# The second layer of a mixture of experts in Strassen form for its last 1024 tokens, with weights split once and kept in DRAM

## The chip, the cores and the metric

The kernel runs on one core of one Trainium2 chip. The metric is the device time of one launch in microseconds (us): a median of 831.98 us over three runs (831.94 to 832.38). The profiled execution, which all rows below come from, took 832.07 us; its span (first to last instruction) is 830.3 us, so 1.77 us lie around the span.

## The reference

Attention over 4 batches of 576 tokens and 8 heads of 64 (half of the heads with a local mask, half with a strided one) gives x, 2304 tokens by 512. Then four experts, each a two-layer network, are summed with weights p per token:

```
x = attention(q, k, v)                      # 2304 x 512, fp32
p = domain_probs / (domain_probs.sum(-1) + 1e-9)
for e in range(4):
    h = max(x @ w1[e], 0)                   # w1[e]: 512 x 1024
    out += p[:, e:e+1] * (h @ w2[e])        # w2[e]: 1024 x 512
```

All of it is fp32. p is not negative, so p times max(h, 0) can be formed before the second layer or applied behind it.

## The kernel before

**Three parts of the tokens.** The 2304 tokens are worked in three parts: the first 384 (beside the attention), a middle part of 896 and a last part of 1024. Each part goes through eight units (expert e, half f of the 1024 hidden columns), so a unit is x times a 512 x 512 block of w1, a relu, and a product with a 512 x 512 block of w2. The last part takes the units in the order 6, 0, 1, 2, 3, 4, 5, 7.

**Split operands.** TensorE (PE) multiplies in float32r. To keep fp32 accuracy each operand is split into a high part (an ACT copy to float32r, `split` L631) and a low part (source minus high, on DVE or POOL, kind "VP" in the plan), and each product is three passes: high by high, high by low, low by high.

**First layer, middle and last part: Strassen.** `plan_unit` (L841) makes seven block products (a11, s1, s2, a12, s3, a22, s4 with b11, t1, t2, b21, t3, t4, b22) instead of eight; each is done for two halves f of its 256 rows by `product` (L829, six matmuls of 448 or 512 columns), so 14 products and 84 matmuls a unit. The weights' combinations and splits are made by DVE, POOL and ACT from the raw block (`plan_w1` L662), in the middle part and again in the last. Some results are copied out of PSUM by ACT (`copy_u`), added by DVE, then relu'd and split into h high (ACT) and h low (DVE).

**Second layer: plain.** `plan_mm2` (L723): a tile of 128 tokens is 12 matmuls of 512 columns with h as the stationary operand (L706); behind it DVE does acc = psum * p + acc (`accumulate`, L715), one instruction a tile. The last part has eight such tiles a unit. At the end each acc goes to DRAM.

**What sets the order.** Every instruction is added to a plan (`Plan`, L33) with an engine, an estimated time, the values read and written, and a priority; `Plan.walk` makes a list schedule, and the engines' instruction streams are written in that order. Engines run their streams in order. PE's products and tiles keep the order in which they are added. "VP" instructions go to DVE or POOL, whichever the plan thinks ends first. Where DVE and POOL overlap, the plan's rule (`took`, L188) charges DVE half of what is left of POOL's instruction:

```
d += min(x / 2, d) if e == "DVE" else min(x, d) * 0.2
```

The SP queue issues all weight loads (`plan_load`: one raw block of 1 MB for w1 and one for w2 a unit) and the outputs, also in order. PSUM has eight banks: four named mo, two sc, two ps.

Of the kernel before, what the change touches and what calls it, by code (L numbers as in the profile page):

```python
# [8 lines left out]
F32 = mybir.dt.float32  # L9
# [23 lines left out]
class Plan:  # L33
# [273 lines left out]
def attn_moe_kernel(  # L307
# [8 lines left out]
    w2: bass.AP,  # L316
    c_masks: bass.AP,
    out: bass.AP,
):
    nc = tc.nc  # L320
    B, H, S, D = 4, 8, 576, 64
    NT, DM = out.shape
    E, _, F = w1.shape
    P = 128
    NKD = DM // P
# [30 lines left out]
    psums = const.tile([P, NTT], F32, name="psums")  # L356
    wz = const.tile([P, 512], BF16, name="wz")

    wq = {n: (big.tile([P, 2, 256], F32R, name=n + "h"), big.tile([P, 2, 256], F32R, name=n + "l")) for n in QUART[:3] + ("s3",)}
    w2h = [big.tile([P, DM], F32R, name=f"w2h{i}") for i in range(NKF)]  # L360
    w2l = [big.tile([P, DM], F32R, name=f"w2l{i}") for i in range(NKF)]
    raws = {1: big.tile([P, NKD, FH], F32, name="raw1"), 2: big.tile([P, NKF, DM], F32, name="raw2")}
    acc = [big.tile([P, DM], F32, name=f"acc{i}") for i in range(TB // P)]
    xr = {"r2": [big.tile([P, TBS[1]], F32, name=f"xr2{c}") for c in range(NKD)]}

    one = tc.tile_pool(name="one", bufs=1)
    op = one.__enter__()
# [294 lines left out]
    def plan_w1(z, step, plain):  # L662
# [16 lines left out]
        combine(t(0), A12, t(1), ["raw1", "ws1"], "ws0", z + 6 * step)  # L679
        plan_quarter(t(0), "ws0", "s4", z + 6 * step)  # L680


    PASS = [(i, c) for i in range(3) for c in range(NKD)]
    PASS0 = [(i, c) for c in KORD for i in range(3)]
# [89 lines left out]
    def open_first():  # L774
        att.__exit__(None, None, None)
        p = ctx.enter_context(tc.tile_pool(name="late1", bufs=1, side="right", reuse_waits="tile"))
        for nm in XOPS:
            xq[nm] = [[p.tile([P, TM], F32R, name=f"{nm}{h}{j}") for j in range(2)] for h in "hl"]
        for nm in ("s1", "s2", "s4"):
            wq[nm] = (p.tile([P, 2, 256], F32R, name=nm + "h"), p.tile([P, 2, 256], F32R, name=nm + "l"))  # L780
        for i in range(3):
            tmp["s", i] = p.tile([P, 2, 256], F32, name=f"tmp{i}")

    def open_second():
        one.__exit__(None, None, None)
        p = ctx.enter_context(tc.tile_pool(name="late2", bufs=1, reuse_waits="tile"))
        late["h"] = [[p.tile([P, TB], F32R, name=f"h{j}{i}") for i in range(NKF)] for j in range(2)]
        late["u"] = [p.tile([P, TM], F32, name=f"u{i}") for i in range(4)]
        late["c"] = [p.tile([P, TM], F32, name=f"c{i}") for i in range(2)]

    def plan_x(part, z, step):

# [48 lines left out]
    def plan_unit(part, u, first, last, z):  # L841
# [31 lines left out]
        for n, (a, b, keys, first_in) in enumerate(SEQ):  # L873
            for f in range(2):
                key = keys[f]
                zz = z + (2 * n + f) * PM
                need = [a + "h", a + "l"] + [f"{b}{h}{j}" for h in "hl" for j in range(2)]
                add("PE", PM, lambda a=a, b=b, f=f, key=key, first_in=first_in: product(a, b, f, key, first_in, TH),
                    need, [key], zz, key if first_in else None, True, 6 * TH)
                ze = zz + PM  # L880
                if n == 0:
                    copy_u("p1", f, key, ze)
                elif n == 2:
                    copy_u("u2", f, key, ze)
# [34 lines left out]
        plan_pair(n)  # L919
    add("SP", 0.4, load_pr, (), ["prs"], 8, xfer=((0.1, 128),))  # L920
    add("DVE", 1.0, normalize, ["prs"], ["pr"], 30)

    for u in range(NU):
        z = Z0 + ZU * u
# [17 lines left out]
    for part, seq in ((1, first_order), (2, second_order)):  # L942
        PM = pm_of(part)
        w1_at = 14 * PM + 2 * PT * (TBS[part - 1] // P)
        for i, u in enumerate(seq):
            if part == 1 and i == 0:
                plan_w1(z, 2 * PM, False)
            elif i > 0:
                plan_load(1, u, z - w1_at + 9)
                plan_w1(z, 2 * PM, True)  # L950
                plan_load(2, u, z - w1_at + 17)
                plan_w2(z + 14 * PM)
# [96 lines left out]
```

## Time and profile before

| what | value |
|---|---|
| median of 3 runs | 831.98 us |
| profiled execution | 832.07 us, span 830.3 us |
| first part with the attention | 0 to 210.0 us |
| middle part, 8 units of 36.1 us | 210.0 to 498.7 us |
| last part, 8 units of 40.95 us | 498.7 to 826.3 us |
| PE busy | 822.8 us of the span |
| DVE, ACT, POOL busy | 496.3, 322.4, 213.2 us |
| moved by DMA | 70.6 MB |

Busy time is that of an engine's instructions; idle time of an engine that nobody waits for costs nothing. In the rows below L with a number is the line of the kernel before.

### The profile page before, as it was taken

The page shows a single profiled execution, that of the slowest core. Times are in us where ns is not written, and L with a number is a line of the kernel's source. Part 1 is how long each engine was busy: PE and PEld are TensorE (multiplying, and loading weights), DVE is VectorE, ACT ScalarE, POOL GpSimd, SP SyncE. Part 2 cuts the span into 40 slices and gives each one's busy share as a digit, 9 for nine tenths or more (in the row PEclk, how much of TensorE's full clock was granted, in tenths as well). Part 3 has the DMA queues.
Part 4 walks back from the last instruction along what each step waited for, and adds up shares of the span by engine and source line. Part 5 has one row for each costly group of instructions (what it writes and reads, how often), then busy time and mean ns, then how long its engine had stood idle before and what let it go on. Part 6 is the DMA issues. An engine that isn't in the chain of part 4 may idle for free.

```text
span 830.3 us, 13407 instructions
## 1 busy us (share of the span) xinstructions
PE 822.8 (99%) x5492; PEld 702.5 (85%) x5495; DVE 496.3 (60%) x773; ACT 322.4 (39%) x607; POOL 213.2 (26%) x185
## 2 busy tenths in 40 slices
PE   8999999999999999999999999999999999999998
PEld 5888988998988888898888888888888888888886
DVE  6977877855646465574647685464646464646342
ACT  3644546542514334161433525161515151515130
POOL 5421134841223131231315271121211111111000
PEclk9999999999999999999999999999999999999999
DMA  9675532343012111121211110111112020201002
GB/s 341 238 282 180 202 143 95 106 147 114 28 49 101 51 52 51 51 58 52 94 51 51 51 71 19 52 54 48 58 44 69 33 80 23 89 12 52 1 8 95
DMA packets 33230, 70.60 MB, mean 85 GB/s; under 512 B 1936, under 2 KB 2320, under 8 KB 33168
## 3 DMA queue, kind: packets, MB, share of 16 engines
q1 hardware_dynamic: 33024, 69.66, 24.0%
q8 instruction: 43, 0.70, 0.3%
q14 instruction: 19, 0.16, 0.1%
q10 hardware_dynamic: 144, 0.08, 0.0%
HBM read 65.01 MB, written 4.72 MB: 84 GB/s over the span
## 4 chain that ended last, share of the span: by engine, by line
PE 96%; DMA 2%; DVE 1%; POOL 0%; ACT 0%; issue 0%; ACTq 0%
PE mo L706 28%; PE mo L834 17%; PE ps L706 10%; PE sc L706 10%; PE ps L834 9%; PE sc L834 9%; PE mo L690 8%; PE ps L551 1%; PE sc L469 1%; PE ps L559 1%; DMA raw<-in_w 1%; PE ps L523 1%; PE sc L464 1%; DMA both<-c_masks 0%; DVE pmS L486 0%
## 5 line engine op out<-in xcount | busy, mean ns | idle before, releaser
L706 PE MATMUL mo<-w2h,h 128*128 128x512 f32 (+1 forms) x488 | 159.2, 387 | 0.0
L634 ACT ACTIVATE w2h<-raw 128x512 fp32r<-128x512 f32 x88 | 54.6, 631 | 249.5 <-PE ps L706 104.6
L715 DVE SCALAR_TENSOR_TENSOR acc<-mo,pr,acc 128x512 f32<-128x512 f32 x74 | 55.2, 746 | 88.1 <-PE mo L706 87.4
L706 PEld LDWEIGHTS mo<-w2h,h 128*128 128x128 f32 x488 | 91.4, 188 | 18.7
L706 PE MATMUL mo<-w2l,h 128*128 128x512 f32 (+1 forms) x244 | 94.6, 388 | 0.0
L697 DVE SCALAR_TENSOR_TENSOR h<-c,h 128x448 fp32r<-128x448 f32 (+1 forms) x96 | 90.9, 977 | 6.0 <-ACT h L694 3.6
L706 PE MATMUL ps<-w2h,h 128*128 128x512 f32 x240 | 78.8, 389 | 0.0
L706 PE MATMUL sc<-w2h,h 128*128 128x512 f32 (+1 forms) x240 | 77.8, 386 | 0.0
L635 POOL TENSOR_TENSOR w2l<-raw,w2h 128x512 fp32r<-128x512 f32 x24 | 32.7, 1366 | 151.1 <-ACT w2h L634 150.5
L706 PE MATMUL mo<-w2h,hs 128*128 128x512 f32 x192 | 63.3, 397 | 0.0
L694 ACT ACTIVATE h<-c 128x448 fp32r<-128x448 f32 (+1 forms) x96 | 55.6, 601 | 13.3 <-DVE c L866 11.7
L706 PEld LDWEIGHTS mo<-w2l,h 128*128 128x128 f32 x244 | 45.8, 188 | 9.3
L706 PEld LDWEIGHTS ps<-w2h,h 128*128 128x128 f32 x240 | 45.0, 188 | 9.3
L706 PEld LDWEIGHTS sc<-w2h,h 128*128 128x128 f32 x240 | 44.9, 188 | 9.1
L635 DVE TENSOR_TENSOR w2l<-raw,w2h 128x512 fp32r<-128x512 f32 x64 | 45.5, 742 | 9.5 <-ACT w2h L634 9.5
L635 POOL TENSOR_TENSOR s3l<-tmp,s3h 128x512 fp32r<-128x512 f32 x14 | 18.3, 1305 | 115.3 <-ACT s3h L634 107.2
L853 ACT ACTIVATE u<-mo 128x448 f32<-128x448 f32 (+1 forms) x48 | 27.4, 572 | 51.4 <-PE mo L834 50.8
L706 PE MATMUL ps<-w2l,h 128*128 128x512 f32 x120 | 46.7, 389 | 0.0
L706 PE MATMUL sc<-w2l,h 128*128 128x512 f32 (+1 forms) x120 | 46.3, 386 | 0.0
L706 PEld LDWEIGHTS mo<-w2h,hs 128*128 128x128 f32 x192 | 36.0, 188 | 7.9
L715 DVE SCALAR_TENSOR_TENSOR acc<-ps,pr,acc 128x512 f32<-128x512 f32 x27 | 20.3, 751 | 36.7 <-PE ps L706 36.6
L866 DVE TENSOR_TENSOR c<-mo,u 128x448 f32<-128x448 f32 (+1 forms) x48 | 31.1, 648 | 16.0 <-issue 8.1
(279 smaller groups left out, 1710.1 us busy)
## 6 DMA issues: line engine op xcount, KB each, us to landing
raw<-in_w SPq DMA_DIRECT2D x44, 1024.0 KB, 5.2
qkS<-in_qk_strided SPq DMA_DIRECT2D x16, 329.0 KB, 7.7
vstL<-in_v_local SPq DMA_DIRECT2D x8, 640.0 KB, 8.2
out<-acc SPq DMA_DIRECT2D x17, 256.0 KB, 2.0
vstS<-in_v_strided SPq DMA_DIRECT2D x8, 384.0 KB, 8.1
qkL<-in_qk_local SPq DMA_DIRECT2D x8, 336.0 KB, 6.9
qkL<-in_qk_local SPq DMA_DIRECT2D x8, 272.0 KB, 6.3
out<-acc SPq DMA_DIRECT2D x2, 128.0 KB, 1.7
```

What stands on the lines that cost most here:

```text
L464: nc.tensor.matmul(s[64 * h + 32 * i:64 * h + 32 * i + 32, o:o + W], qkv[a, t:t + 32], qkv[a, t + nq + 1:t + nq + 1 + W], start=True, stop ...
L469: nc.tensor.matmul(s[a, o:o + W], lhsT, rhs, start=True, stop=True)
L634: add("ACT", 0.62, lambda: nc.scalar.activation(out=hi(), in_=src(), func=AF.Copy), need, [name + "h"], z)
L635: add("VP", VP, lambda e: engine(e).tensor_tensor(out=lo(), in0=src(), in1=hi().bitcast(F32), op=ALU.subtract), need + [name + "h"], [name ...
L690: nc.tensor.matmul(pt[:, 0:TA], w[:, c % 2, (f % 2) * P:(f % 2) * P + P], (xl if i == 1 else xh)[c], start=j == 0, stop=j == 11)
L694: nc.scalar.activation(out=dst(), in_=src(), func=AF.Relu)
L697: nc.vector.scalar_tensor_tensor(out=dst(), in0=src(), scalar=0.0, in1=hi().bitcast(F32), op0=ALU.max, op1=ALU.subtract)
L706: nc.tensor.matmul(pt, ht[f][:, ts], wt[f][:, cs], start=j == 0, stop=j == 11)
L715: nc.vector.scalar_tensor_tensor(out=a, in0=pt, scalar=sc, in1=a, op0=ALU.mult, op1=ALU.add)
L834: nc.tensor.matmul(pt, wq[a][i == 2][:, j, f * P:f * P + P], xq[b][i == 1][j][:, 0:TH], start=bool(first) and n == 0, stop=True, skip_grou ...
L853: add("ACT", TH / 1200 + 0.18, lambda: nc.scalar.activation(out=late["u"][i][:, 0:TH], in_=held[key][:, 0:TH], func=AF.Copy), [key, "late2 ...
L866: add("DVE", TH / 960 + 0.14, lambda: nc.vector.tensor_tensor(out=late["c"][c][:, 0:TH], in0=held[key][:, 0:TH], in1=late["u"][i][:, 0:TH] ...
```

## The change

**Middle part.** The split weight operands are now stored. After each unit's seven w1 operands are split, SP writes each (high and low together, 512 KB) to DRAM (`plan_keep1`, not for unit 6, whose operands stay in place). `plan_keep2` does the same for w2: three operands are written straight from the split w2 block (rows of 1 KB), and the other four are formed by four "VP" combinations and four splits through two buffers wv0 and wv1. So a middle unit has 14 more DMAs, 8 more "VP" instructions and 4 more ACT copies (unit 6 seven DMAs fewer).

**Last part.** No raw weights are loaded and none are split. SP reads the seven w1 operands of a unit back into place (`reload`) and the seven w2 operands through a ring of four buffers (`plan_ring`). The second layer is Strassen as well, with w2 as the stationary operand, so the output is turned (512 x 1024, turned back on the host): 14 products of six matmuls (`plan_o`) instead of eight tiles of twelve. h becomes q = max(h, 0) * p on DVE, with p spread over all partitions (`pb`, by DMA from a turned copy `dp` in DRAM, once an expert), and q's seven combinations are formed and split (`plan_t`). Each product of the second layer is added to acc by DVE. `TURN` interleaves: a turn is the h products of one unit, two of the next unit's ("next P2", "next s1"), and then the seven o products.

```diff
+    wt = {n: big.tile([P, 2, 2, 256], F32R, name=n) for n in QUART[:3] + ("s3",)}
+    wq = {n: (t[:, 0], t[:, 1]) for n, t in wt.items()}
...
+    def plan_keep1(u, z):
+        for n, nm in enumerate(QUART):
+            add("SP", 0.4, lambda nm=nm: nc.sync.dma_start(out=d1[u, nm], in_=wt[nm].bitcast(F32)), [nm + "h", nm + "l"], [f"d1{u}{nm}"],
+                z + n, xfer=((1.45, 128),))
...
+        def keep(n, nm):
+            v = n % 2
+            split(t((0, 1, 2, 0)[n]), f"ws{(0, 1, 2, 0)[n]}", lambda: late["wv"][v][:, :, 0], lambda: late["wv"][v][:, :, 1], f"wv{v}", z + n * step)
+            add("SP", 0.4, lambda: nc.sync.dma_start(out=d2[u, nm], in_=late["wv"][v].bitcast(F32)), [f"wv{v}h", f"wv{v}l"], [f"d2{u}{nm}"],
+                z + n * step + 2, xfer=((1.45, 128),))
...
+    STEPS = {"P2": ("a12", "b21", "b", 1), "s1": ("s1", "t1", "c", 1), "P1": ("a11", "b11", "a", 1), "s4": ("s4", "b22", "c", 0),
+             "s2": ("s2", "t2", "a", 0), "s3": ("s3", "t3", "a", 0), "a22": ("a22", "t4", "a", 0)}
+    TURN = ("h P1", "h s4", "h s2", "next P2", "h s3", "next s1", "h a22", "o P1", "o s1", "o s2", "o s4", "o s3", "o P2", "o a22")
...
+            if nm:
+                i = late[nm, f]
+                add("DVE", DD, lambda: nc.vector.tensor_tensor(out=q(), in0=src(), in1=late["u"][i], op=ALU.add),
+                    [key, f"u{i}", "late3"], [tok], zz)
+            from_q = bool(nm)
+            add("DVE", DD, lambda: nc.vector.scalar_tensor_tensor(
+                out=q(), in0=q() if from_q else src(), scalar=0.0, in1=late["p"][:, c * TH2:c * TH2 + TH2], op0=ALU.max, op1=ALU.mult),
...
+            elif step == "s3":
+                sub(q[0, 0, j], q[1, 1, j], q[0, 0, j], z)
+                put(q[0, 0, j], "t2", j, z)
+                put(q[1, 1, j], "b22", j, z + 2 * dz)
+                sub(q[0, 1, j], q[1, 1, j], q[0, 1, j], z + 4 * dz)
+                put(q[0, 1, j], "t3", j, z + 4 * dz)
...
+            key = ({"a": "sc", "b": "ps", "c": "mo"}[kk], "o" + kk, u, f)
...
+            add("PE", dz, lambda f=f, key=key: product(
+                [late["ring"][slot][:, :, h] for h in range(2)], late["T"][b], f, key, first_in, TH2),
+                need, [key], zz, key if first_in else None, True, 6 * TH2)
...
+                add("DVE", DD, lambda i=i, key=key: nc.vector.tensor_tensor(
+                    out=acc[i], in0=held[key][:, 0:TH2], in1=acc[i], op=ALU.add), [key], tok, zz + dz)
...
-            elif part == 2:
-                plan_x(2, z, 2 * PM)
-            plan_unit(part, u, i == 0, i == NU - 1, z)
-            z += w1_at
...
+        plan_keep2(u, z + 14 * PM, 2 * PM)
+        z += w1_at
+    plan_x(2, z, 2 * pm_of(2))
...
+    plan_second()
```

**DVE in the last part.** Before, the stretch of a unit from the second half of its h products to the first tiles; c is an h product with a parked one added, h0 and h1 are h's high and low parts, mo, ps and sc are PSUM banks.

```order
L697 SCALAR_TENSOR_TENSOR h12_2771<-c0_2777,h02_2767 128x512
L697 SCALAR_TENSOR_TENSOR h13_2772<-c1_2778,h03_2768 128x512
L697 SCALAR_TENSOR_TENSOR h12_2771<-mo_5249,h02_2767 128x512
L697 SCALAR_TENSOR_TENSOR h13_2772<-ps_5261,h03_2768 128x512
L866 TENSOR_TENSOR c0_2777<-mo_5270,u2_2775 128x512
L866 TENSOR_TENSOR c1_2778<-ps_5279,u3_2776 128x512
L697 SCALAR_TENSOR_TENSOR h10_2769<-c0_2777,h00_2765 128x512
L697 SCALAR_TENSOR_TENSOR h11_2770<-c1_2778,h01_2766 128x512
L715 SCALAR_TENSOR_TENSOR acc0_94<-mo_5382,pr_72,acc0_94 128x512
```

After, from s3's first h product to the first read of an o product (acc0 from sc); q is max(h, 0) * p, v a parked product, T... the o operands (l low, h high).

```order
L928 TENSOR_TENSOR q110_5072<-ps_5659,v2_5057 128x512
L931 SCALAR_TENSOR_TENSOR q110_5072<-q110_5072,pb_5065 128x512
L928 TENSOR_TENSOR q111_5073<-ps_5667,v3_5058 128x512
L960 TENSOR_TENSOR q000_5066<-q110_5072,q000_5066 128x512
L931 SCALAR_TENSOR_TENSOR q111_5073<-q111_5073,pb_5065 128x512
L956 TENSOR_TENSOR Tt2l0_5092<-q000_5066,Tt2h0_5090 128x512
L960 TENSOR_TENSOR q001_5067<-q111_5073,q001_5067 128x512
L956 TENSOR_TENSOR Tb22l1_5085<-q111_5073,Tb22h1_5083 128x512
L931 SCALAR_TENSOR_TENSOR q100_5070<-ps_5659,pb_5065 128x512
L956 TENSOR_TENSOR Tt2l1_5093<-q001_5067,Tt2h1_5091 128x512
L931 SCALAR_TENSOR_TENSOR q101_5071<-ps_5667,pb_5065 128x512
L1005 TENSOR_TENSOR acc0_80<-sc_5798,acc0_80 128x512
```

Before, an instruction that reads a bank had at most two instructions with both inputs in SBUF ahead of it in such a stretch; now seven stand ahead of the read of sc.

**POOL beside it.** Before, POOL's whole unit in the last part:

```order
L635 TENSOR_TENSOR s3l_83<-tmp2_2199,s3h_82 128x512
L635 TENSOR_TENSOR a22l_81<-raw1_92,a22h_80 128x512
L635 TENSOR_TENSOR s4l_2196<-tmp0_2197,s4h_2195 128x512
L639 TENSOR_TENSOR tmp1_2198<-tmp0_2197,raw1_92 128x512
L635 TENSOR_TENSOR w2l1_89<-raw2_93,w2h1_85 128x512
```

After, POOL's whole turn; the first needs q110, which is the second DVE row above.

```order
L960 TENSOR_TENSOR q010_5068<-q110_5072,q010_5068 128x512
L956 TENSOR_TENSOR Tb22l0_5084<-q110_5072,Tb22h0_5082 128x512
L956 TENSOR_TENSOR Tt3l0_5096<-q010_5068,Tt3h0_5094 128x512
L960 TENSOR_TENSOR q011_5069<-q111_5073,q011_5069 128x512
L956 TENSOR_TENSOR Tt3l1_5097<-q011_5069,Tt3h1_5095 128x512
L956 TENSOR_TENSOR Tb21l0_5080<-q100_5070,Tb21h0_5078 128x512
L960 TENSOR_TENSOR q100_5070<-q100_5070,q000_5066 128x512
L960 TENSOR_TENSOR q101_5071<-q101_5071,q001_5067 128x512
```

POOL has gone from five instructions a unit, spread over it, to eight in a row behind s3.

**SP in the middle part.** Before, SP issued two loads a unit and nothing else there:

```order
L624 DMA raw1_92<-in_w1 128x4x512
L624 DMA raw2_93<-in_w2 128x4x512
```

After, one unit (d1 and d2 are the DRAM copies of the w1 and w2 operands):

```order
L634 DMA raw2_202<-in_w2 128x4x512
L695 DMA d11s2_101<-s2_2297 128x1024
L695 DMA d11a12_98<-a12_77 128x1024
L695 DMA d11s3_102<-s3_79 128x1024
L695 DMA d11a22_99<-a22_78 128x1024
L695 DMA d11s4_103<-s4_2298 128x1024
L634 DMA raw1_201<-in_w1 128x4x512
L715 DMA d21s1_149<-wv0_2877 128x1024
L715 DMA d21s2_150<-wv1_2878 128x1024
L715 DMA d21s3_151<-wv0_2877 128x1024
L715 DMA d21s4_152<-wv1_2878 128x1024
L704 DMA d21a11_146<-w2t_200 512x1x256
```

Behind these come two more of the w2 block and two of the next unit's w1; the two raw loads of a unit now stand between 14 writes.

## Rows read from the trace of the kernel before

**Rows 1.** The page: engines' busy time; the chain that ended last, by engine.
```profile
PE 822.8 (99%) x5492; PEld 702.5 (85%) x5495; DVE 496.3 (60%) x773; ACT 322.4 (39%) x607; POOL 213.2 (26%) x185
...
PE 96%; DMA 2%; DVE 1%; POOL 0%; ACT 0%; issue 0%; ACTq 0%
```

**Rows 2.** What PE waited for, longest in total first: us, times, longest.
```profile
PE mo L961 <- DVE wz L964: 1.2, 1, 1.2
```

**Rows 3.** Windows: a middle unit, the last middle unit, a unit of the last part.
```profile
318.30:354.40 36.10, 36.10 (x170) 31.52 (x169) 20.52 (x29) 13.72 (x26) 9.46 (x8) 1.00 0.18 59
462.60:498.70 36.10, 36.10 (x170) 31.52 (x168) 27.40 (x33) 15.74 (x30) 19.50 (x13) 1.00 0.21 74
558.99:599.94 40.95, 40.95 (x182) 33.79 (x181) 22.61 (x33) 14.53 (x26) 6.87 (x5) 1.00 0.16 52
```

**Rows 4.** The chain through that last unit: start, us, engine, bank, line, matmuls.
```profile
558.99 2.73 PE mo L706 x12
...
578.05 2.72 PE sc L706 x12
580.77 1.39 PE mo L834 x6
...
598.59 1.36 PE ps L834 x6
```

**Rows 5.** Timeline of DVE there: start, us, line, out<-in; x2 is two instructions.
```profile
558.45 0.68 DVE L866 TENSOR_TENSOR c<-mo,u 128x512 f32<-128x512 f32 x1
559.05 0.68 DVE L866 TENSOR_TENSOR c<-sc,u 128x512 f32<-128x512 f32 x1
...
586.52 0.69 DVE L635 TENSOR_TENSOR s1l<-tmp,s1h 128x512 fp32r<-128x512 f32 x1 [1.04 <-ACT s1h L634]
587.32 0.69 DVE L639 TENSOR_TENSOR tmp<-raw,tmp 128x512 f32<-128x512 f32 x1
...
592.98 1.29 DVE L697 SCALAR_TENSOR_TENSOR h<-c,h 128x512 fp32r<-128x512 f32 x2
...
596.25 2.04 DVE L697 SCALAR_TENSOR_TENSOR h<-c,h 128x512 fp32r<-128x512 f32 x2 [0.34 <-ACT h L694]
598.21 0.68 DVE L697 SCALAR_TENSOR_TENSOR h<-mo,h 128x512 fp32r<-128x512 f32 x1
```

**Rows 6.** Timeline of POOL there.
```profile
595.83 1.30 POOL L635 TENSOR_TENSOR s3l<-tmp,s3h 128x512 fp32r<-128x512 f32 x1 [14.31 <-ACT s3h L634]
598.51 1.29 POOL L635 TENSOR_TENSOR a22l<-raw,a22h 128x512 fp32r<-128x512 f32 x1 [1.39 <-ACT a22h L634]
```

**Rows 7.** Timeline at the end of the middle part, DVE.
```profile
487.23 1.71 DVE L639 TENSOR_TENSOR tmp<-xr,tmp 128x512 f32<-128x512 f32 x1
488.86 1.78 DVE L639 TENSOR_TENSOR tmp<-raw 128x512 f32<-128x512 f32 x1
```

**Rows 8.** The same stretch, POOL.
```profile
490.05 1.74 POOL L808 TENSOR_TENSOR t4l<-tmp,t4h 128x512 fp32r<-128x512 f32 x1
```

**Rows 9.** Timeline of ACT in the unit of the last part.
```profile
582.25 0.60 ACT L853 ACTIVATE u<-mo 128x512 f32<-128x512 f32 x1 [0.82 <-PE mo L834]
```

**Rows 10.** Timeline of DVE at the end of the span.
```profile
826.67 0.48 DVE L715 SCALAR_TENSOR_TENSOR acc<-mo,pr,acc 128x256 f32<-128x256 f32 x1 [0.95 <-PE mo L706]
```

**Rows 11.** The page: DMA issues, KB each, us from issue to landing.
```profile
raw<-in_w SPq DMA_DIRECT2D x44, 1024.0 KB, 5.2
...
out<-acc SPq DMA_DIRECT2D x17, 256.0 KB, 2.0
...
out<-acc SPq DMA_DIRECT2D x2, 128.0 KB, 1.7
```

**Rows 12.** Windows at the start: the share and rate of DMA stand last.
```profile
0.00:20.00 20.00, 16.94 (x345) 11.85 (x348) 12.36 (x30) 7.78 (x17) 10.39 (x25) 1.00 0.93 339
```

**Rows 13.** Timeline of DVE in a middle unit, at the end of its products.
```profile
334.57 0.61 DVE L697 SCALAR_TENSOR_TENSOR h<-mo,h 128x448 fp32r<-128x448 f32 x1
```

**Rows 14.** The chain there: the first tile of the second layer.
```profile
335.38 2.74 PE ps L706 x12
```

More of the change, by code (lines that the diff above doesn't have):

```diff
@@ L321, in attn_moe_kernel @@
     B, H, S, D = 4, 8, 576, 64
-    NT, DM = out.shape
+    NT, DM = B * S, out.shape[1]
     E, _, F = w1.shape
@@ L779, in open_first @@
         for nm in ("s1", "s2", "s4"):
-            wq[nm] = (p.tile([P, 2, 256], F32R, name=nm + "h"), p.tile([P, 2, 256], F32R, name=nm + "l"))
+            wt[nm] = p.tile([P, 2, 2, 256], F32R, name=nm)
+            wq[nm] = (wt[nm][:, 0], wt[nm][:, 1])
+        held["tmp"] = tc.tile_pool(name="late1t", bufs=1, side="right", reuse_waits="tile")
+        p = held["tmp"].__enter__()
         for i in range(3):
@@ new lines, in plan_p, with load, plan_second, reload @@
+    def plan_p(u, z):
+        e = units[u][0]
+        def load():
+            s = dp[:, :]
+            src = bass.AP(s.tensor, s.offset + e * P, [[0, P], [E * P, TBS[1] // P], [1, P]])
+            nc.sync.dma_start(out=late["p"].rearrange("p (t c) -> p t c", c=P), in_=src)
+        add("SP", 0.4, load, ["dp", "late3"], ["pb"], z, xfer=((1.5, 1024),))
+    def plan_second():
+        dz = pm_of(2)
+        zz = z
+        seq = second_order
+        plan_p(seq[0], zz)
+        for step in ("P2", "s1"):
+            plan_h(seq[0], step, zz, dz)
+            zz += 2 * dz
+        def reload(step, v, z):
+            nm = STEPS[step][0]
+            add("SP", 0.4, lambda: nc.sync.dma_start(out=wt[nm].bitcast(F32), in_=d1[v, nm]), [f"d1{v}{nm}"], [nm + "h", nm + "l"],
+                z, xfer=((1.45, 128),))
+        if NU > 1:
+            reload("P2", seq[1], zz)
+            reload("s1", seq[1], zz)
+        for i, u in enumerate(seq):
+            v = seq[i + 1] if i + 1 < NU else None
+            w = seq[i + 2] if i + 2 < NU else None
+            slots = {}
+            fetch = list(FETCH)
+            for _ in range(RING):
+                st = fetch.pop(0)
+                slots[st] = plan_ring(u, st, zz)
+            for what in TURN:
+                kind, step = what.split()
+                if kind == "next":
+                    if v is None:
+                        continue
+                    plan_h(v, step, zz, dz)
+                    if w is not None:
+                        reload(step, w, zz + 6 * dz)
+                elif kind == "h":
+                    plan_h(u, step, zz, dz)
+                    if step in ("P1", "s2", "s3", "a22"):
+                        plan_t(step, zz + 2 * dz, dz)
+                    if v is not None:
+                        reload(step, v, zz + 6 * dz)
+                    if step == "a22" and v is not None and units[v][0] != units[u][0]:
+                        plan_p(v, zz + 4 * dz)
+                else:
+                    plan_o(u, step, slots[step], i == 0, i == NU - 1, zz, dz)
+                    if fetch:
+                        st = fetch.pop(0)
+                        slots[st] = plan_ring(u, st, zz)
+                zz += 2 * dz
@@ L921, in attn_moe_kernel, with turn_pr @@
     add("DVE", 1.0, normalize, ["prs"], ["pr"], 30)
+    key = ("ps", "pr")
+    def turn_pr():
+        nc.tensor.transpose(bank(key)[0:TBS[1] // P * E, 0:P], pr[:, T0[2] // P:NTT, :].rearrange("p t e -> p (t e)"), ident)
+    add("PE", 0.11, turn_pr, ["pr", "ident"], [key], 60, key, cols=256)
+    add("DVE", 0.25, lambda: nc.vector.tensor_copy(out=prT, in_=held[key][0:TBS[1] // P * E, 0:P]), [key], ["prT"], 60)
+    add("SP", 0.4, lambda: nc.sync.dma_start(out=dp, in_=prT), ["prT"], ["dp"], 70, xfer=((0.1, 128),))
     for u in range(NU):
@@ L941, in attn_moe_kernel @@
     second_order = [NU - 2] + list(range(NU - 2)) + [NU - 1]
[L942 to L952, printed above, removed]
-            elif part == 2:
-                plan_x(2, z, 2 * PM)
-            plan_unit(part, u, i == 0, i == NU - 1, z)
-            z += w1_at
+    PM = pm_of(1)
+    w1_at = 14 * PM + 2 * PT * (TBS[0] // P)
+    for i, u in enumerate(first_order):
+        if i == 0:
+            plan_w1(z, 2 * PM, False)
+        else:
+            plan_load(1, u, z - w1_at + 9)
+            plan_w1(z, 2 * PM, True)
+            plan_load(2, u, z - w1_at + 17)
+            plan_w2(z + 14 * PM)
+        if u != NU - 2:
+            plan_keep1(u, z + 4)
+        plan_unit(1, u, i == 0, i == NU - 1, z)
+        plan_keep2(u, z + 14 * PM, 2 * PM)
+        z += w1_at
+    plan_x(2, z, 2 * pm_of(2))
+    add("DVE", 0.0, open_third, [f"{nm}l{j}" for nm in XOPS for j in range(2)],
+        ["late3", "raw1", "raw2"] + [t for t in list(plan.writer) if isinstance(t, str) and (
+            t[0] == "H" or t[:2] in ("r2", "ws", "wv", "w2") or t in [f"{x}{i}" for x in "uc" for i in range(4)])], z)
+    plan_second()
     def idle(n, tag):
```

144 lines of the change are left out of this document (128 added, 16 removed).

## Prediction

> **What bounds the kernel now.** I read the page's busy times and its chain first: PE is busy 99% of the span, and 96% of the chain that ended last is PE [rows 1]. The list of PE's waits confirms it: the longest is 1.2 us, at the start [rows 2], and its seven rows add up to 3.8 us. In the windows the middle part and the last part show PE busy for all of each unit, with DVE busy 20.5 of 36.1 us and 22.6 of 40.95 us, POOL 9.5 and 6.9 us [rows 3]. So a matmul taken away is time gained, as long as DVE, POOL and the DMAs still serve PE in time.
>
> **The change, part by part.**
>
> *Matmuls of the last part.* In the chain a tile of the second layer is 12 matmuls in 2.72 to 2.73 us, eight tiles from 558.99 to 580.77, so 21.78 us; then 14 products of six matmuls from 580.77 to 599.95, so 19.18 us, 1.37 us each [rows 4]. The new second layer is 14 products of the same shape. A unit goes from 21.78 + 19.18 = 40.96 to 2 x 19.18 = 38.36 us: 2.60 us less, and over eight units 20.8 us less. No other matmul is removed; PE gains one small transpose in the first part, where it still waits at times, so I put it at nothing (bounds: 0.5 us either way, since the plan's order around it shifts).
>
> *The tail.* Now DVE reads a half tile behind the last matmul for 0.48 us, and 128 KB takes 1.7 us to land [rows 10, 11]. After, DVE reads 512 columns (0.68 us [rows 5]) and 256 KB takes 2.0 us [rows 11]: 0.2 + 0.3, with two such outputs behind each other about +0.6 us (bounds 0 to 1.5).
>
> *DVE against POOL in the last part.* Here is the cost that decides. DVE instructions that follow each other start 0.60 us apart when independent, and 0.80 us when one needs the other (586.52 and 587.32) [rows 5]. Two relu instructions with both inputs in SBUF take 1.29 us alone, but 2.04 us where POOL runs from 595.83 to 597.13: the first waits for POOL's end [rows 5, 6]. One that reads PSUM takes 0.68 us although POOL runs beside it (598.21 against 598.51) [rows 5, 6]. Where both queues are full, each instruction on either side takes about 1.7 us (DVE 1.71 and 1.78, POOL 1.74): they alternate [rows 7, 8]. So a meeting costs DVE all that is left of POOL's 1.30 us.
>
> The Trainium skill says the same and more sharply (SBUF — State Buffer, section "Who interferes with whom"): a VectorE instruction with two SBUF inputs and a GpSimd one that reads SBUF exclude each other for the whole instruction, whichever issues first; the rows agree. By it the sum is the one below, 822.7 us. The kernel's own plan charges only half of what is left; by that the steady turns would not stall and the last by about half, and the sum would be some 815 us.
>
> I write one turn of the last part by hand, from the start of h P1, with slots of 2.74 us (two products). The read of s3's first half starts at 12.75 on DVE. From there to the read of the first o product (acc0 from sc) DVE has twelve instructions: at 0.60 us each, 0.20 for one dependence and 0.68 for the last, it would end at 20.2. The o product s2 adds into the same bank in slot 9 and can issue at about 24.5, so there are 4.3 us of cover. But seven of the twelve have both inputs in SBUF, and five POOL instructions of 1.30 us (q010, b22 low, t3 low, q011, t3 low) run just there, interleaved by ACT's copies of 0.60 us [rows 9]. Walking the two queues by hand, the five meetings and the waits for ACT add 4.9 us: the read ends at 25.1, and PE waits some 0.6 us; at o s4 the same thing costs another 0.2. That is 0.8 us in each of six steady turns, 4.8 us. Bounds a turn: zero, if the meetings fall better than I drew them, and 5 x 1.30 - 4.3 = 2.2 us if each costs its full length, so 0 to 13 us; I take my drawing, because its two inputs (whole exclusion, 0.60 pitch) are the rows. The first turn has no such stall: POOL has five instructions there, and ACT makes the first copies into acc. All other readings of a turn have cover: P1's bank is read by 3.5 us and needed at 5.5, s2's by 9.0 and needed at 11.0, and behind o s3 a turn leaves DVE nothing but reads of PSUM.
>
> *The last turn.* Without the next unit's two products (5.48 us) the same reads are due 5.5 us earlier. By the same drawing a22's second half waits 1.7 us for the read of s3 (it stands behind two meetings on t1), o s2 waits about 3 us more for acc0 (behind t2's last low part), and o s2's second half and o s3 another 1.5: 6 us (bounds 1, if the meetings cost nothing, and 9).
>
> *DMA in the last part.* Seven reloads and seven ring loads of 512 KB a turn are 7.3 MB in 38 us, 192 GB/s; the first window moved 339 GB/s at a share of 0.93 [rows 12]. A reload has from a product of this turn to the same product of the next, the ring some 8 us where 256 KB takes 2.0 and 1024 KB 5.2 [rows 11]. Hidden; if a ring load were late, PE would wait for the rest of it.
>
> *The middle part.* No PE instruction changes. A unit's DMA grows from 2 MB to 14 x 0.52 + 2 x 1.05 = 9.4 MB, in 36.1 us 261 GB/s, 77% of what rows 12 show. SP issues in order, so a raw load stands behind writes that wait for their split: w1's behind s4's low part. Its data are used only in the next unit's splits, some 20 us later, so 5.2 us [rows 11] even doubled is covered; w2's is used a unit later. On DVE and POOL eight instructions come on top of 20.5 and 9.5 us in 36.1 [rows 3]. Four of POOL's fall into the products' second half, beside DVE's relu instructions; the last h low part of the first tiles ended at 335.18 there, and the tile that begins at 335.38 uses it in its last matmul, 2.5 us in [rows 13, 14]. One more meeting (1.30 us) leaves 1.4 us of cover. So nothing; without that cover up to 0.5 us a unit, 4 us in all. The last middle unit, where x is combined and split for the last part, had DVE at 27.4 us and POOL at 19.5 [rows 3] and its last split ended at 491.8 [rows 8], 6.9 us ahead of need; four weight preparations go and eight instructions of keep2 come, within that.
>
> **The sum**, against the profiled execution: 832.07 - 20.8 + 0.6 + 4.8 + 6.0 = 822.7 us. That execution is 0.1 us above the median of 831.98, so I say 822.6 us.
>
> **Rivals.**
>
> *DVE keeps up.* If ACT's waits and POOL's meetings fall on each other rather than add, the 4.3 us of cover hold and only the last turn stalls by about 2 us: 832 - 20.8 + 0.6 + 2 = 814 us. For it: DVE's instructions of a turn at 0.60 us are 42 x 0.60 = 25 us of 38, which is slack enough. Against it: the twelve that matter are in one run, beside five in a row on POOL.
>
> *The read of o P1 becomes the bound (slower).* In every steady turn the sc bank is read late: the place is o s2. From 20.8 - 0.6 - 6 = 14.2 us over seven turns, 2.0 us a turn, the gain is gone. If every meeting costs the full 1.30 (2.2 us) and the reads behind it, o s4's and o s3's, are pushed as well (0.5 us), a turn loses 2.7 us: 832 - 20.8 + 0.6 + 6 + 7 x 2.7 = 837 us. For it: alternation at 1.7 us an instruction is seen [rows 7, 8]. Against it: PSUM reads pass POOL freely, which breaks the alternation.
>
> *The writes bind the middle part (slower still).* If the 16 transfers of a unit were worked one after another, each would take its landing time: 2.0 + 2 x 0.3 = 2.6 us for 512 KB by the step from 128 to 256 KB, and 5.2 for a raw block [rows 11]: 14 x 2.6 + 2 x 5.2 = 46.8 us a unit instead of 36.1, 86 us in all: about 908 us. The Trainium skill (DMA: Bandwidth & Descriptors, section "Anatomy of one DMA") puts a transfer at about 2.0 us plus its bytes at 436 GB/s, which taken one by one is an estimate of 54 us a unit. Against it: 339 GB/s in the first window can only come from several in flight.
>
> **How the numbers follow.** Forecast (stalls of 5 to 16 us, 817 to 829 us): 0.57. DVE keeps up: 0.22. The read becomes the bound: 0.13. The writes bind: 0.05. The rest, 0.03, is a mix near no change. About 0.2%, 1.7 us, is what a measurement can tell from no change. Faster: 0.56 + 0.22 = 0.78. Slower: 0.10 of the 0.13 and 0.05, 0.15. Within 0.2%: 0.07. The range takes in the keeping-up case and the lower part of the late read: 812 to 835 us; it leaves out some 0.16.
>
> **What would show it.** In the profile after: turns of 38.4 us plus a stall; PE's waits headed by "DVE acc", at o s2, some 0.8 us and six or seven times; a longer group in the last turn, 6 us; middle units still 36.1 us; DVE rows with two SBUF inputs at 1.2 to 1.9 us beside POOL. I am wrong if PE's waits in the last part name DMA, if middle units grow, or if the last part's turns are at 38.4 throughout.

## The result and the profile after

The changed kernel takes 824.85 us (median of four runs, 823.37 to 826.38) against 831.97: a ratio of 0.9913, 95% interval 0.9892 to 0.9935. Forecast were 822.6 us, 812 to 835. The profiled run took 825.78 us, with a span of 824.0.

The page of after, first row and chain by engine, answers to [rows 1]:

```profile
PE 810.3 (98%) x5385; PEld 686.0 (83%) x5388; DVE 625.2 (76%) x892; ACT 330.6 (40%) x616; POOL 308.3 (37%) x243
...
PE 95%; DVE 1%; DMA 1%; issue 1%; POOL 1%; ACT 0%; POOLq 0%; ACTq 0%
```

PE's busy time fell by 12.5 us, DVE's and POOL's rose by 129 and 95, and PE still carries the chain. The fall is less than the 20.8 us of matmuls that the forecast took away: a product that is held up inside counts as busy (38.80 us in a steady turn of after, 38.23 in one without a stall, both below). The stage borders come from the chain (start, us, what): before, its first products of the middle part and of the last part are

```profile
209.98 1.21 PE mo L834 x6
...
498.86 1.39 PE mo L834 x6
```

and in after

```profile
213.82 1.21 PE mo L897 x6
...
503.34 5.50 PE mo L897 x24
...
820.27 0.69 DVE acc L1005
```

The last of these rows answers to [rows 10]. The first part grew by 3.84 us, the middle part by 0.64 (288.88 to 289.52). From 498.86 to 826.67 the last part took 327.81 us before; from 503.34 to 820.27 it takes 316.93, 10.88 less. The sum, -6.4, is the profiled runs' difference, 6.3, to a tenth.

PE's waits in after (us in total, times, longest), for [rows 2]:

```profile
PE sc L897 <- issue: 3.6, 7, 2.2
PE ps L897 <- DVE q L928: 1.5, 1, 1.5
```

The first row, seven times, stands at o s2 once in each of six steady turns and once in the last; I had expected its releaser to be named as DVE's acc. The second belongs to the last turn.

Windows of after, in the columns of [rows 3]: a middle unit, a steady turn, the last turn, and two short stretches that come up below (the third column from the end is the granted clock; 0.50 is the lower of its two levels, 1.2 GHz, and 1.00 the upper, 2.4 GHz):

```profile
320.00:356.10 36.10, 36.10 (x170) 31.52 (x169) 27.30 (x34) 16.28 (x29) 14.42 (x10) 1.00 0.71 257
...
586.18:625.22 39.04, 38.80 (x170) 31.38 (x169) 32.65 (x42) 11.86 (x20) 11.99 (x8) 1.00 0.59 202
781.40:820.24 38.84, 35.12 (x145) 27.63 (x143) 30.31 (x40) 9.46 (x16) 15.56 (x10) 0.96 0.28 98
62.00:64.00 2.00, 2.00 (x8) 2.00 (x7) 0.60 (x2) 0.00 (x0) 0.00 (x0) 0.50 0.08 26
806.00:808.00 2.00, 2.00 (x6) 1.54 (x6) 2.00 (x4) 0.00 (x0) 1.92 (x2) 0.50 0.00 0
```

The middle unit is still 36.10 us, with PE never idle, though its DMA share went from 0.18 to 0.71. A steady turn has 0.24 us without PE, and its chain shows where:

```profile
586.18 2.77 PE ps L897 x12
...
608.10 2.72 PE mo L897 x12
610.82 0.24 issue
611.05 3.00 PE sc L897 x12
614.06 3.01 PE mo L897 x12
...
625.22 1.85 PE ps L897 x8
```

At 610.82 PE comes to o s2 and stands idle; o s2 and o s4 take 3.0 us in the chain where the other products take 2.7. 0.24 + 0.28 + 0.29 is 0.8 us over a turn without a stall (38.23 in a run below). By the starts of their matmuls, o s2 begins 0.4 us late and takes 0.1 us longer, and o s4 is held up by 0.3 us in its second half. DVE (first fence) and POOL (second) just ahead of that, for [rows 5 to 8]:

```profile
602.27 1.78 DVE L931 SCALAR_TENSOR_TENSOR q<-q,pb 128x512 f32<-128x512 f32 x1
603.97 1.78 DVE L956 TENSOR_TENSOR Tt2l<-q,Tt2h 128x512 fp32r<-128x512 f32 x1
605.67 1.78 DVE L960 TENSOR_TENSOR q<-q,q 128x512 f32<-128x512 f32 x1
607.37 0.68 DVE L956 TENSOR_TENSOR Tb22l<-q,Tb22h 128x512 fp32r<-128x512 f32 x1
...
610.28 1.27 DVE L1005 TENSOR_TENSOR acc<-sc,acc 128x512 f32<-128x512 f32 x2
```

```profile
601.75 1.74 POOL L956 TENSOR_TENSOR Tb22l<-q,Tb22h 128x512 fp32r<-128x512 f32 x1
...
605.16 1.74 POOL L960 TENSOR_TENSOR q<-q,q 128x512 f32<-128x512 f32 x1
607.64 1.56 POOL L956 TENSOR_TENSOR Tt3l<-q,Tt3h 128x512 fp32r<-128x512 f32 x1 [0.74 <-ACT Tt3h L955]
```

While POOL works without a break, DVE's instructions with two SBUF inputs start 1.70 us apart; in POOL's pause, and when they read PSUM, 0.60. The read of o P1's bank begins 24.1 us into the turn; o s2 starts 24.87 in.

### The profile page after: what moved, and what is told of

Same layout as the page of the kernel before. It is cut to its first block, busy times and chain, and to the rows that moved or that the text cites. A ratio compares the mean times of both kernels' runs of the same rounds, so it can differ in the third digit from the quotient of the medians.

```text
span 824.0 us, 13898 instructions
## 1 busy us (share of the span) xinstructions
PE 810.3 (98%) x5385; PEld 686.0 (83%) x5388; DVE 625.2 (76%) x892; ACT 330.6 (40%) x616; POOL 308.3 (37%) x243
## 3 DMA queue, kind: packets, MB, share of 16 engines
HBM read 108.00 MB, written 59.79 MB: 204 GB/s over the span
## 4 chain that ended last, share of the span: by engine, by line
PE 95%; DVE 1%; DMA 1%; issue 1%; POOL 1%; ACT 0%; POOLq 0%; ACTq 0%
PE mo L897 21%; PE mo L750 17%; PE ps L897 16%; PE sc L897 15%; PE mo L734 8%; PE ps L750 5%; PE sc L750 5%; PE ps L561 2%; PE sc L479 1%; PE ps L533 1%; PE sc L474 1%; DMA qkL<-in_qk_local 1%; PE ps L569 1%; POOL q L960 1%; PE mo L1205 1%
## 5 line engine op out<-in xcount | busy, mean ns | idle before, releaser
L960 POOL TENSOR_TENSOR q<-q,q 128x512 f32<-128x512 f32 x31 | 44.8, 1445 | 211.9 <-DVE q L931 186.2
L750 PE MATMUL mo<-w2t,h 128*128 128x512 f32 x336 | 80.8, 389 | 0.0
L750 PEld LDWEIGHTS mo<-w2t,h 128*128 128x128 f32 x336 | 63.1, 188 | 13.0
L750 PE MATMUL mo<-w2t,hs 128*128 128x512 f32 x288 | 69.9, 395 | 0.0
L750 PEld LDWEIGHTS mo<-w2t,hs 128*128 128x128 f32 x288 | 53.0, 188 | 11.0
L741 DVE SCALAR_TENSOR_TENSOR h<-c,h 128x448 fp32r<-128x448 f32 x48 | 59.6, 1268 | 2.4 <-ACT h L738 1.0
L645 POOL TENSOR_TENSOR a<-raw,a 128x512 fp32r<-128x512 f32 x22 | 34.1, 1549 | 59.6 <-DVE c L1097 44.9
L645 POOL TENSOR_TENSOR w2t<-raw,w2t 128x512 fp32r<-128x512 f32 x21 | 30.2, 1447 | 46.6 <-ACT w2t L644 44.0
L734 PE MATMUL mo<-xh,a 128*128 128x384 f32 x192 | 46.7, 345 | 0.0
L931 DVE SCALAR_TENSOR_TENSOR q<-q,pb 128x512 f32<-128x512 f32 x48 | 41.1, 857 | 1.1
L750 PE MATMUL ps<-w2t,h 128*128 128x512 f32 x168 | 40.4, 389 | 0.0
L750 PE MATMUL sc<-w2t,h 128*128 128x512 f32 x168 | 40.4, 389 | 0.0
L645 DVE TENSOR_TENSOR w2t<-raw,w2t 128x512 fp32r<-128x512 f32 x39 | 33.9, 897 | 4.5 <-ACT w2t L644 4.5
```

Source lines behind the costliest of these rows:

```text
L645: add("VP", VP, lambda e: engine(e).tensor_tensor(out=lo(), in0=src(), in1=hi().bitcast(F32), op=ALU.subtract), need + [name + "h"], [name ...
L734: nc.tensor.matmul(pt[:, 0:TA], w[:, c % 2, (f % 2) * P:(f % 2) * P + P], (xl if i == 1 else xh)[c], start=j == 0, stop=j == 11)
L741: nc.vector.scalar_tensor_tensor(out=dst(), in0=src(), scalar=0.0, in1=hi().bitcast(F32), op0=ALU.max, op1=ALU.subtract)
L750: nc.tensor.matmul(pt, ht[f][:, ts], wt[f][:, cs], start=j == 0, stop=j == 11)
L931: add("DVE", DD, lambda: nc.vector.scalar_tensor_tensor(out=q(), in0=q() if from_q else src(), scalar=0.0, in1=late["p"][:, c * TH2:c * TH ...
L960: add("VP", VP, lambda e: engine(e).tensor_tensor(out=dst[0](), in0=a[0](), in1=b[0](), op=ALU.subtract), [a[1], b[1]], [dst[1]], zz)
```

## The experiments

Each ran beside the kernel before on one chip; the ratio is to that kernel, with its 95% interval in brackets, and after's 824.85 us is the comparison within the study.

**1. The turning of the first part's output, put behind the attention.** The PE transpose, the DVE copy and the DMA `dp<-prT` (L1153 to L1160) stand behind the attention's plan, with its due time and token:

```
-    add("PE", 0.11, turn_pr, ["pr", "ident"], [key], 60, key, cols=256)
+    add("PE", 0.11, turn_pr, ["pr", "ident", "late1"], [key], z + 60, key, cols=256)
...
```

Expected: 

> The whole turning of the first part's output (PE transpose, DVE copy, the DMA that reads the turned tile back) is put behind the attention instead of in the middle of the first part. Theory (the 3.8 us that the first part takes longer than before come from that DMA, which stands 7 us in SP's queue ahead of the loads of the attention's operands, and from the wait and the fall of the granted clock to 0.61 that follow at 60 us): the middle part starts near 210 instead of 213.8, the clock stays at 1.0 from 55 to 70 us, and the time is 821 to 822 (3 to 4 us under the profiled run of after, 2 to 3 under its median). Rival (the first part's loss has to do with the tiles' sizes and buffers that the change altered, or with the run): middle part still starts near 213 and the time stays within 0.15% of after's 824.9.

Measured: 821.6 us (821.53 to 822.23), ratio to before 0.9874 [0.986, 0.9888]. The first part's 3.8 us do hang on this turning: the middle part now begins where it began before (210.06 below, 209.98 before).

**2. Only its DMA put there;** transpose and copy stay.

```
-    add("SP", 0.4, lambda: nc.sync.dma_start(out=dp, in_=prT), ["prT"], ["dp"], 70, xfer=((0.1, 128),))
+    add("SP", 0.4, lambda: nc.sync.dma_start(out=dp, in_=prT), ["prT", "late1"], ["dp"], z + 70, xfer=((0.1, 128),))
```

Expected: 

> Only the DMA that reads the turned tile back is moved behind the attention; the transpose on PE and the copy on DVE stay where they are. If SP's queue is the cause of the first part's 3.8 us, it gains as much as the kernel that moves the whole chain (821 to 822, middle part from about 210). If the cause is the transpose's place in PE's order, nothing is gained (about 825, middle part from about 213.8).

Measured: 824.07 us (823.2 to 824.12), 0.9902 [0.9889, 0.9914]: no gain beyond the spread of after's runs. The first products of the middle part (timeline of PE) in experiment 1, experiment 2 and after:

```profile
210.06 0.57 PE L897 MATMUL mo<-b11h,a 128*128 128x448 f32 x2
```

```profile
212.13 0.57 PE L897 MATMUL mo<-b11h,a 128*128 128x448 f32 x2
```

```profile
213.66 0.57 PE L897 MATMUL mo<-b11h,a 128*128 128x448 f32 x2
```

So my theory of SP's queue falls: without the DMA there, 2.07 us of the loss remain. They come with the transpose's and copy's place in the plan (which of the two was not separated), which deals out the whole first part in another order: from 35 to 40 us PE works 98 matmuls in the kernel before and in experiment 1, 64 in experiment 2 and 60 in after. In its first 200 us PE is idle for 5.5 us in experiment 2 and for 3.6 us in experiment 1. The chain of experiment 2 has a wait there that experiment 1 has not (first fence), and after has the same one (second):

```profile
59.86 0.63 issue
60.48 0.49 PE sc L479 x9
60.98 2.31 PE mo L734 x12
```

```profile
59.73 0.75 issue
60.48 0.49 PE sc L479 x9
60.97 3.84 PE mo L734 x12
```

In after the next twelve matmuls take 3.84 instead of 2.31 us: the granted clock fell there (0.50 in the window from 62). That is the other 1.53. Of after's four runs the two with a mean clock of 1.000 took 823.4 and 823.9, the other two 825.8 and 826.4; experiment 2's 823.2 to 824.1 is no gain over the first two. Whether the DMA has a part in the fall no run shows.

**3. All splits and differences of the last part's turns on DVE.** In `plan_t`, at the low parts (here) and at the differences:

```
-            add("VP", VP, lambda e: engine(e).tensor_tensor(out=lo(), in0=src(), in1=hi().bitcast(F32), op=ALU.subtract),
-                [tok, f"T{nm}h{j}"], [f"T{nm}l{j}"], zz)
+            add("DVE", VP[0], lambda: nc.vector.tensor_tensor(out=lo(), in0=src(), in1=hi().bitcast(F32), op=ALU.subtract),
+                [tok, f"T{nm}h{j}"], [f"T{nm}l{j}"], zz, two=True)
```

Expected: 

> In the last part's turns POOL gets no subtraction: all of the splits and differences are DVE's, so a turn has 16 DVE instructions ahead of the read of o P1's bank, where after has 12 and POOL's 4 to 6 beside them. Theory (DVE and POOL exclude one another on SBUF, and DVE's subtractions stretch from 0.6 to 1.2 us and more beside POOL's): 16 x 0.6 us and the 12.7 us up to the first of them end before the 24.5 us at which o s2 wants the bank, so the steady turns lose their stall (38.4 instead of 39.0), the last turn is 2 to 4 us shorter, and the time is 817 to 821. Rival (the mere number of instructions in DVE's queue sets the read of the bank): the stall grows by 4 x 0.6 = 2.4 us in each of six turns, and the time is 835 to 842.

Measured: 817.61 us (817.41 to 818.7), 0.9829 [0.9816, 0.9842]. The whole of the extra work is on DVE, and it is ready earlier. From the timeline of DVE in the same stretch of a turn:

```profile
600.28 0.68 DVE L956 TENSOR_TENSOR Tt2l<-q,Tt2h 128x512 fp32r<-128x512 f32 x1
600.88 0.68 DVE L956 TENSOR_TENSOR Tb22l<-q,Tb22h 128x512 fp32r<-128x512 f32 x1
...
605.41 1.28 DVE L956 TENSOR_TENSOR Tt3l<-q,Tt3h 128x512 fp32r<-128x512 f32 x2
606.61 0.68 DVE L1005 TENSOR_TENSOR acc<-sc,acc 128x512 f32<-128x512 f32 x1
```

Independent instructions start 0.60 us apart throughout. The read of o P1's bank begins 23.0 us into this turn (from 583.60) instead of 24.1, although from the read of s3's first bank on 16 instructions stand ahead of it instead of 11. The window of the turn, beside after's of 586.18:

```profile
583.60:621.83 38.23, 38.23 (x169) 31.48 (x169) 31.70 (x50) 11.61 (x20) 0.00 (x0) 1.00 0.60 206
```

DVE is busy for 31.70 us with 50 instructions; in after it was busy for 32.65 us with 42, and POOL for 11.99 us beside it. The chain's steady turns (545.36 to 774.76 in six) are 38.23 us instead of 39.04, and none has a wait. The last turn, 774.76 to 811.78, is 37.02 instead of 38.84; the granted clock stays at 1.00 in it. The exclusion is the cause of the stall, and the length of DVE's queue is not.

**4. The planner charges a meeting of DVE and POOL in full** (in `took`):

```
-                    d += min(x / 2, d) if e == "DVE" else min(x, d) * 0.2
+                    d += min(x, 1.3) if e == "DVE" else min(x, d)
```

Expected: 

> The planner that deals the work of the last part's turns out to DVE and POOL charges an overlap of the two to DVE up to 1.3 us instead of up to its own duration's share, so POOL gets fewer pieces; the order of the rest follows from its plan. Theory of the exclusion: the steady turns' stall of 0.68 goes down to 0 to 0.4, last turn 1 to 3 us less: 819 to 823. Rival (the stall is set by the length of DVE's queue): as many instructions as after stand ahead of the read of the bank, so the stall is unchanged and the time is 824 to 826.

Measured: 829.64 us (828.92 to 833.62, 12 runs), 0.9981 [0.997, 0.9993]: slower than either theory said. The rule holds for the whole program, so the first part was dealt out anew as well: the middle part begins 2.2 us later than in after, and the mean granted clock was 0.57 from 24 to 34 us. The turns got longer too (39.80 us for the one from 549.84): PE waits 0.8 us six times at a bank sc, by the list for ACT's Tb21h, and 3.4 us once in the last turn. It tells nothing of the exclusion, since too much moved at once.

**5. Fewer writes.** The writes in `plan_keep1` and `plan_keep2` are made for the first unit only, and all reads name its tiles:

```
-        add("SP", 0.4, lambda: nc.sync.dma_start(out=late["ring"][i].bitcast(F32), in_=d2[u, nm]), [f"d2{u}{nm}", "late3"], [f"ring{i}"],
+        add("SP", 0.4, lambda: nc.sync.dma_start(out=late["ring"][i].bitcast(F32), in_=d2[NU - 1, nm]), [f"d2{NU - 1}{nm}", "late3"], [f"ring{i}"],
...
```

Expected: 

> Of the 105 writes of split weight operands to DRAM only the 14 of the first unit are made; all units of the last part read these (so the output is not the reference's; 91 writes of 256 KB are left out, the reads are as many as in after). Theory (the writes are hidden): the middle part takes 288.7 to 289.5 us against after's 289.5, the turns of the last part are 38.3, 39.0 and 38.8 as in after, and the time is 823 to 826. Rival (the writes cost something, by DMA time that the loads lack or by buffers that stay taken): the middle part gets shorter than 288.7 or the turns shorter than 38.3, and the time falls below 822.

Measured: 824.12 us (823.36 to 827.74), 0.9908 [0.989, 0.9927]: the same as after. 12.08 MB were written instead of 59.79 (91 writes of 0.52 MB less; the 256 KB of the expectation is half their size), and the middle part took 289.53 us (211.81 to 501.34) against 289.52:

```profile
211.81 1.21 PE mo L897 x6
...
501.34 5.50 PE mo L897 x24
```

The writes are hidden entirely. The middle part's 0.64 us is therefore not theirs; the chain of both profiles has a split for the stored operands (L645, DVE, 1.76 us, at 222.97 in after, beside one on POOL) in the first unit's products, and PE waits 0.4 us at the end of that chain.

**6. Experiments 1 and 3 together.**

Expected: 

> Both edits that gained alone: the turning of the first part's output behind the attention, and the splits of the last part's turns on DVE alone. They act in different stages, so the gains should add up: 817.6 less some 2.3 us (what the first part loses at a granted clock of 1.0) is 815.3; 814.5 to 816. If the two hang together (the planner's order of the last part altered by the later chain), 816.5 to 818.

Measured: 815.8 us (815.42 to 816.46), 0.9802 [0.9785, 0.9819]. From the two medians 814.4 would follow, if the gains just added. The rest is in the last turn: 38.49 us (771.95 to 810.44) against 37.02 in experiment 3, with the mean granted clock at 0.68 from 795 to 800 us. Nothing shows that the two edits hang together.

**7. The read of o P1's bank due six slots earlier,** POOL as in after (in `plan_o`):

```
                 add("DVE", DD, lambda i=i, key=key: nc.vector.tensor_tensor(
-                    out=acc[i], in0=held[key][:, 0:TH2], in1=acc[i], op=ALU.add), [key], tok, zz + dz)
+                    out=acc[i], in0=held[key][:, 0:TH2], in1=acc[i], op=ALU.add), [key], tok, zz + dz - (6 * dz if step == "P1" else 0))
```

Expected: 

> After with one thing altered: the read of o P1's bank gets a due time six slots earlier, so that it stands 2 to 4 instructions further ahead in DVE's order; POOL keeps its part of the splits. Theory (o s2 waits in the steady turns because this read is late): the stall of 0.68 us goes from each of six turns, last turn 1 to 3 us shorter, 818 to 821. Rival (the stall belongs to DVE's whole work of a turn, and moves to the splits that now stand behind the read, before o s4 or o s3): turns stay at 39.0, 823.5 to 826.

Measured: 820.48 us (819.43 to 821.91), 0.9859 [0.9841, 0.9877]. In the chain of the turn from 583.56 the place has no wait:

```profile
608.19 2.72 PE sc L897 x12
610.91 2.72 PE mo L897 x12
```

A turn is 38.30 us (583.56 to 621.86). So the row that PE's list calls "issue" was the wait for that read. The last turn did not get shorter as I had said: 39.82 us (775.26 to 815.08) instead of 38.84. PE waits there 2.8 us for another of DVE's reads, one product later, and the mean granted clock is 0.76 from 800 to 805 us.

**8. The same on top of experiment 6.**

Expected: 

> The two edits that gained alone, and the read of o P1's bank with a due time six slots earlier. The steady turns have no stall left to lose; in the last turn 1.4 us of PE's waits stand in the profile of the kernel with the splits on DVE, before that read. If that read is what is waited for, 814 to 815; if the splits are, it is as without the edit, 815 to 816.

Measured: 820.12 us (819.91 to 820.57), 0.9855 [0.9836, 0.9874]: worse than experiment 6 by 4.3 us, which neither theory gave. In the chain the stall of the steady turns is back, one product later, at o s4 (3.02) and at o s3, ahead of which PE stands idle:

```profile
567.71 2.72 PE sc L897 x12
570.43 3.02 PE mo L897 x12
573.45 0.18 issue
573.63 2.98 PE sc L897 x12
```

The operands of both are long ready (the last low parts of b22 and t3 end at 562.6 and 568.1). What ends just before PE goes on is the read of the bank that each writes into: o s1's second bank mo, and o s2's first bank sc. DVE in the same turn (it begins at 543.08):

```profile
563.67 0.69 DVE L1005 TENSOR_TENSOR acc<-sc,acc 128x512 f32<-128x512 f32 x1 [0.49 <-PE sc L897]
...
571.04 0.68 DVE L1005 TENSOR_TENSOR acc<-mo,acc 128x512 f32<-128x512 f32 x1
...
572.85 1.28 DVE L1005 TENSOR_TENSOR acc<-sc,acc 128x512 f32<-128x512 f32 x2
```

Without POOL's meetings DVE reaches the early read before o P1 is done and idles there for 0.49 us; the two reads behind it begin 27.96 and 29.77 us into the turn, in experiment 3 27.21 and 29.02, three quarters of a microsecond earlier. In experiment 7 DVE came to the same read late enough not to wait. An instruction that is put forward in an engine's queue holds up all that stands behind it.

**9. Experiment 6 with another order of the last turn,** and **10. after with that order alone.** The last unit has no next unit whose P2 and s1 could stand between its own products; o P1 and o s1 are put there:

```
+    LAST = ("h P1", "h s4", "h s2", "o P1", "h s3", "o s1", "h a22", "o s2", "o s4", "o s3", "o P2", "o a22")
-            for what in TURN:
+            for what in TURN if v is not None else LAST:
```

Expected of 9: 

> The kernel with both edits that gained, and in its last turn alone o P1 and o s1 (whose operands are ready early) put in the places where the other turns have the next unit's products, between h s2 and h s3 and between h s3 and h a22. Theory (the last turn loses its 6 us because nothing of a next unit stands between the h and the o products, so PE runs into DVE's reads and splits): the last turn falls from 37 to 38.5 us to 33.5 to 35.5, the granted clock stays at 1.0 to the end, and the time is 812 to 814.5. Rival (DVE's whole work of that turn sets its end, in whatever order PE asks for it): last turn 36 or more, time 815 to 816.5.

Expected of 10: 

> After with the same order of the last turn and nothing else altered: POOL keeps its part of the splits. Theory: the last turn falls from 38.8 us to 34 to 36.5, of which 1.8 is the fall of the granted clock that no longer comes; the other turns stay at 39.0, and the time is 820 to 822.5. Rival (the work of DVE and POOL sets the end): 38 or more, 823.5 to 826.

Measured: experiment 9 812.8 us (812.38 to 813.22), 0.977 [0.9756, 0.9785], the fastest of all and 1.5% under after. Its last turn is 34.14 us (772.42 to 806.56), 2.9 less than experiment 3's, with the clock at 1.00 in both. Experiment 10 824.39 us (824.25 to 825.16), 0.9909 [0.9892, 0.9925], no gain: its last turn is 39.88 us. POOL's pieces meet DVE's in the same way, PE waits 4.0 us at o s2 for t2's high and low parts, and the mean granted clock is 0.69 and 0.63 in the two stretches from 800 to 810 us. DVE (first fence) and POOL (second) of experiment 10 in the last turn:

```profile
796.38 1.78 DVE L932 SCALAR_TENSOR_TENSOR q<-q,pb 128x512 f32<-128x512 f32 x1
798.09 1.78 DVE L957 TENSOR_TENSOR Tt2l<-q,Tt2h 128x512 fp32r<-128x512 f32 x1
```

```profile
795.87 1.75 POOL L957 TENSOR_TENSOR Tb22l<-q,Tb22h 128x512 fp32r<-128x512 f32 x1
797.58 1.75 POOL L957 TENSOR_TENSOR Tt3l<-q,Tt3h 128x512 fp32r<-128x512 f32 x1
```

So the order of PE's work brought 3.0 us where DVE had no POOL beside it, and nothing where it had.

## Why the prediction was right, and where it was not

*Matmuls.* Right. Experiment 3's steady turns without a wait are 38.23 us where 38.36 was said.

*DVE against POOL.* Right in mechanism and nearly in size: the read was drawn to end 25.1 us into the turn and ended at 24.8; a turn was to lose 0.8 us, and 39.04 is 0.81 over the 38.23 of a turn without waits; the first turn has no stall (38.29). Experiments 3 and 7 show the cause from two sides, by taking POOL away and by moving the read. They also bear out the sentence of the Trainium skill that the prediction named (SBUF — State Buffer, "Who interferes with whom"): two DVE inputs in SBUF and POOL beside them, and both alternate at 1.70 us. The parts are a little other than drawn: 0.5 us at o s2 and 0.3 at o s4, where 0.6 and 0.2 were said. The rival "DVE keeps up" fell on this; "the read becomes the bound" was right in its place and wrong in its price.

*The last turn.* Right in mechanism; that the sum fits to a tenth is luck. It was to lose 6.0 us over twelve slots of 2.74 (32.88) and lost 5.96. PE waited 1.5 us at a22 and 2.2 us at o s2, where 1.7 and about 3 were said. But the chain has o s2 there as

```profile
804.79 4.56 PE sc L897 x12
```

where it is 2.72 elsewhere: these 1.84 us lie in a stretch of lower granted clock (0.50 in the window from 806), behind the wait of 2.2 us. I had not counted a clock at all. What the turn is without it shows in experiment 2, whose last turn has the same order and the same waits at a22 and o s2, but a granted clock of 1.00. Its window, and a wait of PE that after does not have, at o s3:

```profile
780.10:818.52 38.42, 34.10 (x144) 26.29 (x143) 30.26 (x40) 9.47 (x16) 15.57 (x10) 1.00 0.27 97
```

```profile
PE sc L897 <- DVE acc L1005: 0.6, 1, 0.6
```

That is 5.5 us over the 32.88, against the 6.0 of the sum. The fall of the clock made the turn only 0.4 us longer, because the waits that come behind o s2 passed under it.

*DMA and the middle part.* Right that the writes are hidden (experiment 5) and the reads too (no wait of PE in the last part names a DMA); raw blocks took 5.9 us to land instead of 5.2. The rival "the writes bind" fell on the middle units, which stayed at 36.10 us. The figure of the Trainium skill that it cites (DMA: Bandwidth & Descriptors, "Anatomy of one DMA") is given there for transfers issued through GpSimd, and these are SP's. By it a raw block is an estimate of 4.4 us; it took 5.2 us before. The middle part's 0.64 us are within the bounds of 0 to 4, 0.4 of them by a wait in one unit that I had not named. *The tail* grew by 0.1 us (from the last read's start to the end of the span, 3.63 and 3.73) instead of 0.6.

*The step that failed* is "one small transpose in the first part, ... so I put it at nothing (bounds: 0.5 us either way)". It cost 3.84 us: about 2.2 by the other order that the plan gives the first part around it, 1.5 by the fall of the clock behind one of the waits. The prediction had said that the plan's order shifts around the transpose, and still bounded the term at half a microsecond. The DMA behind the transpose, which the sum left out, shows no cost by itself (experiment 2). This term and the middle part's 0.6, less the 1.4 by which the last part (0.9) and the tail (0.5) were priced too high, are the 3.1 us between 822.7 and 825.78; the errors partly cancel. Which wait of the first part brings how much of it was not taken apart.

## What to carry to other kernels

An engine that helps can be the brake. Two engines that exclude one another on SBUF may together get less done in time than one: here the one that PE waits for was faster alone, with all the work. Where a planner orders the program, no inserted instruction is free because it is short: compare the start of the next stage, and put it where there is slack. An instruction moved forward in a queue must find its input ready, or it holds up the rest (experiment 8). At a pipeline's last turn, where the next unit's work is missing, reorder what is there to fill the gap.

## What the runs showed of the hardware that was not expected

After short waits of PE the granted clock may fall for some microseconds, and it is not sure to. In after a wait of 0.75 us at 59.73 was followed by a clock of 0.50 from 62 to 64 us, and in experiment 2 one of 0.63 us at the same place by none. At o s2 of the last turn PE waited 2.2 us in after and in experiment 2; the clock was 0.50 from 806 to 808 us in after and stayed at 1.00 in experiment 2. In the last turn of experiment 3 PE waited 1.9 us at o s2 and the clock stayed at 1.00; in experiment 6 it waited 1.8 us at the same product, and from 795 to 800 us the mean clock was 0.68. Where it fell, the products behind the wait took 1.5 to 1.8 us longer. What the stage lost by it is another number: 1.5 us in the last turn of experiment 6 (38.49 against 37.02 in experiment 3), but 0.4 us in that of after (38.84 against 38.42 in experiment 2), where later waits passed under the slower matmuls.
